# The softmax quotient of attention: from one long reciprocal in each block to twelve per partition by small transfers

## The chip, the core and the metric

The kernel runs on one core of a Trainium2 chip. The core's engines work side by side, each through its own instructions in order: TensorE (PE in the profile; its weight loads PEld), VectorE (DVE), ScalarE (ACT), GpSimd (POOL) and SyncE (SP), which here only issues transfers. The metric is the time of one execution in device microseconds; lower is better.

## What is computed

Attention with a hash mask over 2 batches x 8 heads, 768 positions, 64 columns a head; then two expert layers on its output, which the change doesn't touch.

```python
mask = q_bucket[:, :, :, None] == k_bucket[:, :, None, :]
scores = scale * np.matmul(q, k.transpose(0, 1, 3, 2))
scores = np.where(mask, scores, -1000000000.0)
scores = scores - np.max(scores, axis=-1, keepdims=True)
attn = np.exp(scores)
attn = attn / (np.sum(attn, axis=-1, keepdims=True) + 1e-09)
return np.matmul(attn, v).astype(np.float32)
```

The result, turned to x of 1536 x 512, goes through `h = x @ w_in`, a softmax-weighted h with a layer norm, `@ w_out`, and then a gate that sends each row to one of eight experts (two products each).

## The kernel before

Attention works on pairs of heads, j = 0 to 7, two heads side by side on the 128 partitions (64 each). A pair has two blocks, i = 0 and 1, of 384 queries each, and a block has six steps c, of 128 keys each. Scores are kept transposed: keys on partitions, queries along the row. In `run`, the order of the work is written out by hand:

- `score` (each c): TensorE makes scores of 128 keys x 384 queries of both heads into one of three score buffers in PSUM (`wide`), from high and low parts of Q and K and from F, rows that carry the hash mask and the negative row maximum (all L208); ScalarE takes the exponential (L246); on odd c GpSimd adds two of them (L250) and the sum so far (L252), the row sums in the making.
- `rowmax`: for a block to come, TensorE makes scores queries x keys in the same three buffers and VectorE reduces each to its maximum (L219). `submax` (at c = 1) joins the two halves of the keys (L224), clamps and negates (L226), and SP sends the result to one row of Fq by two transfers of 128 pieces (L231).
- at c = 1 of i = 0: `turn` (transposes of the next pair's Q and K, their high and low parts: L170 to L178), `av(j - 1, 1)` (P x V of the block before, L261), `hash` (L185, bits L190), `direct(j - 1, 1)`, `mask` (L197, L201), and SP's loads of V of pair j + 1 and Q and K of pair j + 2. At c = 1 of i = 1: `av(j, 0)`, `direct(j, 0)`, and one of seven clearings of the scratch tensor (SP).
- `direct` makes the quotient: TensorE sums the exponentials over partitions (L273); VectorE copies a column vb that lies beside the product (L280), adds EPS to the sums (L281), takes the reciprocal of all 128 x 384 (L282; within a head all 64 partitions hold the same row), and multiplies (L283, which reads the product in PSUM and adds vb).
- `extra`: the weights of the first expert layer come as float64 and are turned to float32 in 16 pieces, two instructions' turns at the end of every step c from the second block on: ScalarE scales (L392), VectorE shifts (L394), joins (L397) and sets the sign (L401), then ScalarE and GpSimd split into high and low parts (L411, L412; pieces 0 to 7) or ScalarE scales by g (L407; pieces 8 to 15). The transfer of the next piece (512 KB, ScalarE's queue, L376) is issued between two of them.

The three score buffers bind the engines together: TensorE can write the next scores only where VectorE (L219) or ScalarE (L246) has read a buffer.

Of the kernel before, what the change touches and what calls it, by code (L numbers as in the profile page):

```python
# [8 lines left out]
F32 = mybir.dt.float32  # L9
F32R = mybir.dt.float32r  # L10
BF16 = mybir.dt.bfloat16
AF = mybir.ActivationFunctionType
ALU = mybir.AluOpType
AX = mybir.AxisListType
PSUM = bass.MemoryType.PSUM

P = 128
S = 768
D = 64
NC = S // P  # L20
BIG = float(2 ** 40)
E = 8
EPS = 1e-9
NPT = 8
ROWM = 16
HW = S // 2
# [99 lines left out]
class Attention:  # L126
# [85 lines left out]
    def rowmax(self, j, i, c, kh):  # L212
        nc, st = self.nc, self.st[j]
        if (c, kh) == (0, 0):
            st["m", i] = self.sp.tile([P, 3, 2, 2], F32, tag="m", name="m")
        ps = self.wide()
        q, k = slice(i * HW + c, (i + 1) * HW, 3), slice(kh * HW, (kh + 1) * HW)
        self.both(ps, [(st[x + "q"][:, q], st[x + "k"][:, k]) for x in "HF"])
        nc.vector.tensor_reduce(out=st["m", i][:, c, :, kh], in_=ps, axis=AX.X, op=ALU.max)  # L219

    def submax(self, j, i):
        nc, st = self.nc, self.st[j]
        m = st["m", i]
        nc.vector.tensor_tensor(out=m[:, :, :, 0:1], in0=m[:, :, :, 0:1], in1=m[:, :, :, 1:2], op=ALU.max)  # L224
        mr = self.sp.tile([P, 2, 3, 1], F32R, tag="mr", name="mr")
        nc.vector.tensor_scalar(  # L226
            out=mr.rearrange("p h c o -> p c h o"), in0=m[:, :, :, 0:1], scalar1=-BIG / 2, scalar2=-1.0, op0=ALU.max, op1=ALU.mult
        )
        for h in range(2):
            r = D * h + ROWM  # L230
            nc.sync.dma_start(  # L231
                out=st["Fq"][r:r + 1, i * HW:(i + 1) * HW].bitcast(F32),
                in_=mr[:, h, :, 0].bitcast(F32),
            )
# [28 lines left out]
                    start=(c == 0), stop=(c == NC - 1), tile_position=(0, D * h),  # L263
                )

    def direct(self, j, i):
        nc, C, st = self.nc, self.C, self.st[j]
        b, hp = divmod(j, 4)
        ps = self.narrow()
        n = len(st["acc", i])  # L270
        for c in range(n):
            for h in range(2):
                nc.tensor.matmul(  # L273
                    ps[D * h:D * h + D, :], C["ones"], st["acc", i][c][:, h], start=(c == 0), stop=(c == n - 1),
                    tile_position=(0, D * h),
                )
        rb = self.ap.tile([P, HW], F32, tag="rb", name="rb", bufs=2)
        x = st["x", i]
        vb = self.sp.tile([P, 1], F32, tag="vb", name="vb")
        nc.vector.tensor_copy(vb, x[:, HW:HW + 1])  # L280
        nc.vector.tensor_scalar(out=rb, in0=ps, scalar1=EPS, scalar2=None, op0=ALU.add)  # L281
        nc.vector.reciprocal(out=rb, in_=rb)  # L282
        nc.vector.scalar_tensor_tensor(  # L283
            out=self.xT[:, b, hp, i * HW:(i + 1) * HW], in0=x[:, 0:HW], scalar=vb, in1=rb, op0=ALU.add, op1=ALU.mult
        )

    def run(self, n, extra, fills):
        self.last = (n - 1, 1)
        scan = [(j, i, c, kh) for j in range(n) for i in range(2) for c in range(3) for kh in range(2)]

        def scans(m):
            for x in scan[:m]:
                self.rowmax(*x)
            del scan[:m]

        self.turn(0)
        self.hash(0)
        self.mask(0)
        scans(NC)
        self.submax(0, 0)  # L300
        scans(3)
        half = [tuple(range(NC)), (0, 1, 2), (3, 4, 5)]
        for j in range(n):
            nx = j + 1 < n
            for i in range(2):
                more = nx or not i
                for c in range(NC):
                    self.score(j, i, c)
                    scans(((2, 1, 0, 1, 1, 1), (2, 1, 1, 1, 1, 0))[i][c])
                    if c == 1:  # L310
                        if nx or i == 0:
                            self.submax(*((j, 1) if i == 0 else (j + 1, 0)))
                        if i == 0:
                            if nx:
                                self.turn(j + 1)
                            if j:
                                self.av(j - 1, 1, half[0])
                            if nx:
                                self.hash(j + 1)
                            if j:  # L320
                                self.direct(j - 1, 1)
                                self.st.pop(j - 1)
                            if nx:
                                self.mask(j + 1)
                                if j:
                                    self.load(j + 1, "v")
                            if j + 2 < n:
                                self.load(j + 2, "qk")
                        else:
                            self.av(j, 0, half[0])  # L330
                            self.direct(j, 0)
                            if fills:
                                fills.pop(0)()
                    if c == 4 and (j, i) == self.last:
                        self.av(j, 1, half[1])
                    for _ in range(2):
                        if j or i:
                            next(extra, lambda: None)()
        for f in extra:
            f()  # L340
        self.av(n - 1, 1, half[2])
        self.direct(n - 1, 1)


class Weights:
# [10 lines left out]
    def steps(self, pool):  # L356
        nc = self.nc
        todo = [(0, k, h) for k in range(4) for h in range(2)] + [(1, f, 0) for f in range(8)]
        wide = self.src[0].dtype != F32
# [21 lines left out]
        def convert(n):  # L381
            m, k, h = todo[n]
            w = got[n]
            ops = []
            if wide:
                H, L = w[:, :, 1], w[:, :, 0]
                a = pool.tile([P, 512], F32, tag="w", name="w")
                w = self.wo[:, k, :] if m else a
                ai, wi = a.bitcast(I32), w.bitcast(I32)
                V = nc.vector  # L390
                ops = [
                    lambda: nc.scalar.activation(out=a, in_=H.bitcast(F32), func=AF.Copy, scale=2.0 ** -112),  # L392
                    lambda: None,
                    lambda: V.tensor_scalar(  # L394
                        out=ai, in0=ai, scalar1=4, scalar2=1, op0=ALU.logical_shift_left, op1=ALU.logical_shift_right
                    ),
                    lambda: V.scalar_tensor_tensor(  # L397
                        out=ai, in0=L, scalar=29, in1=ai, op0=ALU.logical_shift_right, op1=ALU.bitwise_or
                    ),
                    lambda: None,  # L400
                    lambda: V.scalar_tensor_tensor(  # L401
                        out=wi, in0=H, scalar=-(1 << 31), in1=ai, op0=ALU.bitwise_and, op1=ALU.bitwise_or
                    ),
                    lambda: None,
                ]
            if m:
                ops.append(lambda: nc.scalar.activation(out=w, in_=w, func=AF.Copy, scale=self.g[:, k:k + 1]))  # L407
            else:
                hi, lo = (x[:, k, h * 512:h * 512 + 512] for x in self.wi)
                ops += [  # L410
                    lambda: nc.scalar.copy(hi, w),  # L411
                    lambda: nc.gpsimd.tensor_tensor(out=lo, in0=w, in1=hi.bitcast(F32), op=ALU.subtract),  # L412
                ]
            return ops
# [1 line left out]
        load(0)  # L416
        yield
        for n in range(len(todo)):
            for t, f in enumerate(convert(n)):
                if t == 2:  # L420
                    load(n + 1)
                yield f
            if wide:
                yield from [lambda: None] * (2 if n < 8 else 3)
            if not wide:
                load(n + 1)


def apart(tc, group, ins, gap):
# [735 lines left out]
```

## Time and profile before

| | |
|---|---|
| median of 3 runs (lowest to highest) | 710.62 us (710.31 to 719.96) |
| the profiled execution | 709.09 us |
| its span, first to last instruction | 707.4 us |
| mean granted TensorE clock | 0.939 |
| busy share: TensorE, VectorE, ScalarE, GpSimd | 87%, 68%, 39%, 47% |
| attention stage, from the first row maximum to the first product of the expert layer | 16.4 to 327.0 us |

A line such as L282 is a line of the kernel's source. "Idle before" is time in which the engine did nothing just before the instruction, with what released it behind the arrow. The chain of waits is followed back from the last instruction: at each step to what released it. The granted clock of TensorE is a share of its full speed.

### The profile page before, as it was taken

To read this page: it belongs to the slowest core of one execution; us is meant where nothing else is said; L and a number is where in the kernel's file an instruction comes from. 1 tells how busy PE (TensorE), PEld (TensorE's weight loads), DVE (VectorE), ACT (ScalarE), POOL (GpSimd) and SP (SyncE) were. 2 spreads that over 40 slices of the span, in tenths; PEclk is the share of its full clock that TensorE was granted. 3 is DMA by queue.
4 is the path that set the end of the run, shared out by engine and by line. 5 is a ranking of instruction groups with operands and counts; after the bars stand their busy time and mean duration, and the time that the engine had idled before them with its cause. 6 is when DMAs were issued, how large, how long until landed. Compare 5 with 4: busy or idle time off the path is not lost.

```text
span 707.4 us, 10052 instructions
## 1 busy us (share of the span) xinstructions
PE 615.8 (87%) x3906; PEld 478.7 (68%) x3906; DVE 477.6 (68%) x825; ACT 272.5 (39%) x448; POOL 330.4 (47%) x267
## 2 busy tenths in 40 slices
PE   4788777987788796779699999998899999999995
PEld 2455554544455565556588888887699889988994
DVE  5877867886878877854876787775744664466540
ACT  2344335442525352333323232261343545454530
POOL 1164654865454535554610100333436966696651
PEclk9998989998979998899899999997999999999998
DMA  6141334343343421206000000200466458658400
GB/s 163 24 112 47 82 91 97 90 98 89 97 90 81 108 51 45 78 1 237 1 0 1 1 1 0 75 1 30 167 237 215 164 205 284 213 184 308 144 18 30
DMA packets 77367, 70.11 MB, mean 99 GB/s; under 512 B 46333, under 2 KB 55293, under 8 KB 77312
## 3 DMA queue, kind: packets, MB, share of 16 engines
q1 hardware_dynamic: 72608, 54.69, 26.4%
q10 hardware_dynamic: 2464, 8.39, 3.7%
q0 software_dynamic: 2240, 6.31, 2.5%
q8 instruction: 32, 0.52, 0.3%
q14 instruction: 23, 0.19, 0.1%
HBM read 55.64 MB, written 14.74 MB: 99 GB/s over the span
## 4 chain that ended last, share of the span: by engine, by line
PE 69%; DVE 20%; DMA 3%; POOL 2%; issue 2%; ACT 2%; SPq 1%; POOLq 0%; ACTq 0%; DVEq 0%
PE g L948 13%; PE o L970 13%; PE x L261 9%; PE ps L208 9%; PE y L497 8%; PE h L497 8%; DVE rb L282 4%; DVE m L219 4%; DVE w L397 3%; PE ps L170 2%; PE pm L273 2%; PE t L560 2%; DMA k<-in_k_dram 1%; DVE w L401 1%; DVE w L394 1%
## 5 line engine op out<-in xcount | busy, mean ns | idle before, releaser
L250 POOL TENSOR_TENSOR acc<-pt,pt 128x768 f32<-128x768 f32 x48 | 90.0, 1875 | 141.5 <-ACT pt L246 141.2
L888 POOL TENSOR_TENSOR wl<-ws,wh 128x512 fp32r<-128x512 f32 x80 | 113.5, 1454 | 71.0 <-ACT wh L886 70.5
L246 ACT ACTIVATE pt<-ps 128x768 f32<-128x768 f32 x96 | 76.4, 812 | 98.6 <-PE ps L208 98.6
L219 DVE TENSOR_REDUCE m<-ps 128x2 f32<-128x768 f32 x96 | 88.8, 950 | 25.0 <-PE ps L208 24.6
L886 ACT CAST wh<-ws 128x512 fp32r<-128x512 f32 x128 | 70.3, 618 | 6.0 <-POOL wl L888 4.4
L261 PE MATMUL x<-pt,v 128*64 128x385 f32 x384 | 68.6, 508 | 1.7 <-DVE xT L283 1.7
L208 PE MATMUL ps<-Hq,Hk 64*128 64x384 f32 x192 | 43.4, 447 | 30.5 <-DVE m L219 22.5
L208 PE MATMUL ps<-Hk,Hq 64*128 64x384 f32 x192 | 43.6, 448 | 24.7 <-DVE m L219 22.1
L888 DVE TENSOR_TENSOR wl<-ws,wh 128x512 fp32r<-128x512 f32 x48 | 57.0, 1214 | 11.3 <-ACT wh L886 11.0
L954 DVE SCALAR_TENSOR_TENSOR hl<-g,hh 128x512 fp32r<-128x512 f32 x32 | 22.1, 691 | 62.1 <-ACT hh L953 51.2
L252 POOL TENSOR_TENSOR acc<-acc 128x768 f32<-128x768 f32 x30 | 58.5, 1948 | 2.4
L208 PEld LDWEIGHTS ps<-Hq,Hk 64*128 64x128 f32 x192 | 20.5, 209 | 50.3 <-DVE m L219 27.3
L473 POOL TENSOR_TENSOR xl<-xT,xh 128x512 fp32r<-128x512 f32 x12 | 15.6, 1306 | 82.4 <-ACT xh L488 37.1
L953 ACT ACTIVATE hh<-g 128x512 fp32r<-128x512 f32 x32 | 19.2, 599 | 84.5 <-PE g L948 61.1
L261 PEld LDWEIGHTS x<-pt,v 128*64 128x64 f32 x384 | 27.0, 142 | 36.2 <-issue 35.7
L970 PE MATMUL o<-wh,hh 128*128 128x512 f32 x128 | 51.1, 399 | 0.0
L970 PE MATMUL o<-wl,hh 128*128 128x512 f32 x128 | 50.5, 394 | 0.0
L970 PE MATMUL o<-wh,hl 128*128 128x512 f32 x128 | 50.5, 394 | 0.0
L497 PE MATMUL h<-wi,xh 128*128 128x512 f32 x192 | 50.4, 405 | 0.0
L208 PEld LDWEIGHTS ps<-Hk,Hq 64*128 64x128 f32 x192 | 26.0, 265 | 34.8 <-DVE m L219 28.4
L497 PE MATMUL y<-wo,lh 128*128 128x512 f32 x192 | 47.2, 398 | 0.0
L948 PE MATMUL g<-xh,wh 128*128 128x256 f32 x256 | 41.2, 283 | 0.3 <-ACT xh L917 0.3
(214 smaller groups left out, 1332.5 us busy)
## 6 DMA issues: line engine op xcount, KB each, us to landing
ws<-in_moe_w_dram SPq DMA_DIRECT2D x32, 1024.0 KB
scratch<-zero SPq DMA_DIRECT2D x7, 1030.0 KB
r<-scratch SPq DMA_DIRECT2D x16, 257.5 KB
raw<-in_moe_w_in_dram ACTq DMA_DIRECT2D x8, 512.0 KB
raw<-in_moe_w_out_dram ACTq DMA_DIRECT2D x8, 512.0 KB
q<-in_q_dram SPq DMA_DIRECT2D x16, 192.0 KB
k<-in_k_dram SPq DMA_DIRECT2D x16, 192.0 KB
v<-in_v_dram SPq DMA_DIRECT2D x16, 192.0 KB
```

Of the source, the lines that this page charges most:

```text
L208: self.nc.tensor.matmul(ps[:, h], w[r], x[r], start=(n == 0), stop=(n == len(jobs) - 1), tile_position=(D * h, 0))
L219: nc.vector.tensor_reduce(out=st["m", i][:, c, :, kh], in_=ps, axis=AX.X, op=ALU.max)
L246: nc.scalar.activation(out=pt[:, :, 0:HW], in_=ps, func=AF.Exp, scale=0.125)
L250: nc.gpsimd.tensor_tensor(out=acc, in0=st["pt", i, c - 1][:, :, 0:HW], in1=pt[:, :, 0:HW], op=ALU.add)
L252: nc.gpsimd.tensor_tensor(out=acc, in0=parts.pop(), in1=acc, op=ALU.add)
L261: nc.tensor.matmul(st["x", i][D * h:D * h + D, 0:HW + 1], st["v"][:, c, h, :], st["pt", i, c][:, h, 0:HW + 1], start=(c == 0), stop=(c == ...
L282: nc.vector.reciprocal(out=rb, in_=rb)
L497: nc.tensor.matmul(ps, a[:, k, :], w[j](k), start=(n == 0), stop=(n == len(jobs) - 1))
L886: nc.scalar.copy(hi[:, k, :], t[:, k, :])
L888: eng.tensor_tensor(out=lo[:, k, :], in0=t[:, k, :], in1=hi[:, k, :].bitcast(F32), op=ALU.subtract)
L948: nc.tensor.matmul(ps[:, a, :], w[:, k, f * P:(f + 1) * P], x[:, k, :], start=(n == 0), stop=(n == 11))
L970: nc.tensor.matmul(st["o"][t], h[:, f, t * P:(t + 1) * P], w[:, f % 4, :], start=(f == 0 and n == 0), stop=(f == 7 and n == 2),)
```

## The change

Three parts, all in the attention stage.

The quotient. For pairs 0 to 6 `direct` is taken apart. `evac` copies vb and has ScalarE write the product plus vb from PSUM to SBUF (`xr`). `total` sums and adds EPS. `sums` does both halves of a pair one after the other, and after the second SP gathers the 2 x 768 sums, one partition of each head, to 128 partitions x 12 (`rc`). `recip`, at c = 4 of the next pair's i = 0, takes the reciprocal of these 12 columns; SP writes them to DRAM (`rd`) and reads them back by two broadcasts to 64 partitions each. `norm`, at c = 3 of the next pair's i = 1, multiplies 128 x 768 by 128 x 768. Pair 7 keeps a reciprocal of 128 x 384 in each block (`direct`).

The row maximum. L219 negates, and one scalar_tensor_tensor (two minima) stands for L224 and L226.

The conversions. A piece belongs to a block, from the first block on; the next piece's transfer is issued at the block's start. In i = 0 its instructions stand at the end of c = 0 (ScalarE), in c = 1 after `submax` (L394), and at the end of c = 2 (L397), 3 (L401), 4 and 5. In i = 1: c = 0 (ScalarE), then all three of VectorE in c = 1 between `av` and `evac`, then c = 2 and 3.

```diff
-        nc.vector.tensor_reduce(out=st["m", i][:, c, :, kh], in_=ps, axis=AX.X, op=ALU.max)
+        nc.vector.tensor_reduce(out=st["m", i][:, c, :, kh], in_=ps, axis=AX.X, op=ALU.max, negate=True)
...
-        nc.vector.tensor_tensor(out=m[:, :, :, 0:1], in0=m[:, :, :, 0:1], in1=m[:, :, :, 1:2], op=ALU.max)
         mr = self.sp.tile([P, 2, 3, 1], F32R, tag="mr", name="mr")
-        nc.vector.tensor_scalar(
-            out=mr.rearrange("p h c o -> p c h o"), in0=m[:, :, :, 0:1], scalar1=-BIG / 2, scalar2=-1.0, op0=ALU.max, op1=ALU.mult
+        nc.vector.scalar_tensor_tensor(
+            out=mr.rearrange("p h c o -> p c h o"), in0=m[:, :, :, 0:1], scalar=BIG / 2, in1=m[:, :, :, 1:2],
+            op0=ALU.min, op1=ALU.min,
         )
...
+    def evac(self, j, i):
+        nc, st = self.nc, self.st[j]
+        x = st["x", i]
+        vb = self.sp.tile([P, 1], F32, tag="vb", name="vb")
+        nc.vector.tensor_copy(vb, x[:, HW:HW + 1])
+        if i == 0:
+            st["xr"] = self.ap.tile([P, 2, HW], F32, tag="xr", name="xr", bufs=2)
+        nc.scalar.activation(out=st["xr"][:, i], in_=x[:, 0:HW], func=AF.Identity, bias=vb, scale=1.0)
+
+    def total(self, j, i):
...
+        if i == 0:
+            st["rb"] = self.ap.tile([P, 2, HW], F32, tag="rb", name="rb")
+        nc.vector.tensor_scalar(out=st["rb"][:, i], in0=ps, scalar1=EPS, scalar2=None, op0=ALU.add)
+
+    def sums(self, j, i):
+        nc, st = self.nc, self.st[j]
+        self.total(j, i)
+        if i:
+            st["rc"] = self.sp.tile([P, 12], F32, tag="rc", name="rc")
+            nc.sync.dma_start(out=st["rc"], in_=st["rb"][0:P:D].rearrange("p a n -> p (a n)"))
+
+    def recip(self, j):
+        nc, st = self.nc, self.st[j]
+        nc.vector.reciprocal(out=st["rc"], in_=st["rc"])
+        rd = self.tc.dram_tile([2, S], F32, name=f"rd{j}")
+        nc.sync.dma_start(out=rd.rearrange("h n -> (h n)").rearrange("(p t) -> p t", p=P), in_=st["rc"])
+        rb = st["rb"] = self.ap.tile([P, 2, HW], F32, tag="rd", name="rd")
+        for h in range(2):
+            nc.sync.dma_start(
+                out=rb[D * h:D * h + D].rearrange("p a n -> p (a n)"), in_=rd[h:h + 1].to_broadcast([D, S])
+            )
+
+    def norm(self, j):
+        b, hp = divmod(j, 4)
+        st = self.st.pop(j)
+        o = self.xT[:, b, hp, :].rearrange("p (a n) -> p a n", a=2)
+        self.nc.vector.tensor_tensor(out=o, in0=st["xr"], in1=st["rb"], op=ALU.mult)
+
+    def direct(self, j, i):
...
         nc.vector.reciprocal(out=rb, in_=rb)
-        nc.vector.scalar_tensor_tensor(
-            out=self.xT[:, b, hp, i * HW:(i + 1) * HW], in0=x[:, 0:HW], scalar=vb, in1=rb, op0=ALU.add, op1=ALU.mult
-        )
+        nc.vector.tensor_tensor(out=self.xT[:, b, hp, i * HW:(i + 1) * HW], in0=st["xr"][:, i], in1=rb, op=ALU.mult)
...
                         if i == 0:
+                            some(1)
                             if nx:
                                 self.turn(j + 1)
...
                             if j:
-                                self.direct(j - 1, 1)
-                                self.st.pop(j - 1)
+                                self.evac(j - 1, 1)
+                                self.sums(j - 1, 1)
...
                             self.av(j, 0, half[0])
-                            self.direct(j, 0)
+                            some(3)
+                            self.evac(j, 0)
+                            (self.sums if nx else self.direct)(j, 0)
                             if fills:
                                 fills.pop(0)()
+                    else:
+                        some(1)
+                    if j and (i, c) == (0, 4):
+                        self.recip(j - 1)
+                    if j and (i, c) == (1, 3):
+                        self.norm(j - 1)
                     if c == 4 and (j, i) == self.last:
                         self.av(j, 1, half[1])
-                    for _ in range(2):
-                        if j or i:
-                            next(extra, lambda: None)()
-        for f in extra:
-            f()
+                some(9)
```

`some(m)` issues the next m instructions of the block's piece.

## Rows read from the trace of the kernel before

**Rows 1.** Busy us by stretch: window, length, each engine, clock, DMA share, GB/s.

```profile
105.96:139.83 33.87, 28.81 (x226) 18.41 (x228) 27.40 (x34) 16.05 (x23) 20.52 (x12) 1.00 0.40 98
...
218.56:256.00 37.44, 31.36 (x226) 20.56 (x228) 31.26 (x34) 16.68 (x24) 17.69 (x10) 0.91 0.34 89
...
256.00:296.43 40.43, 30.86 (x215) 21.30 (x216) 30.14 (x33) 15.39 (x22) 18.61 (x11) 0.83 0.28 76
```

**Rows 2.** Chain of waits, attention stage: start us, length us, what.

```profile
47.68 2.56 DVE rb L282
...
63.72 4.03 PE x L261 x24
...
224.81 2.56 DVE rb L282
...
296.43 4.04 PE x L261 x24
...
316.57 2.56 DVE rb L282
```

**Rows 3.** Groups of instructions: total busy us, mean ns, idle before.

```profile
L219 DVE TENSOR_REDUCE m<-ps 128x2 f32<-128x768 f32 x96 | 88.8, 950 | 25.0 <-PE ps L208 24.6
...
L394 DVE TENSOR_SCALAR w<-w 128x512 int32<-128x512 int32 x16 | 15.6, 972 | 6.5 <-ACT w L392 6.5
...
L397 DVE SCALAR_TENSOR_TENSOR w<-raw,w 128x512 int32<-128x512 int32 x16 | 29.7, 1855 | 0.3
```

**Rows 4.** VectorE in order of time: start, length, instruction [idle before].

```profile
186.98 2.55 DVE L282 RECIPROCAL rb<-rb 128x384 f32<-128x384 f32 x1
...
218.12 1.53 DVE L224 TENSOR_TENSOR m<-m 128x6 f32<-128x6 f32 x1
...
223.44 0.62 DVE L190 TENSOR_SCALAR bits<-ps,thr 128x384 bf16<-128x384 f32 x1 [1.48 <-PE ps L185]
...
227.93 0.42 DVE L394 TENSOR_SCALAR w<-w 128x512 int32<-128x512 int32 x1
...
241.65 0.16 DVE L280 COPY vb<-x 128x1 f32<-128x1 f32 x1 [1.39 <-PE x L261]
...
242.30 0.56 DVE L281 TENSOR_SCALAR rb<-pm 128x384 f32<-128x384 f32 x1 [0.49 <-PE pm L273]
...
249.38 0.94 DVE L219 TENSOR_REDUCE m<-ps 128x2 f32<-128x768 f32 x1
...
262.25 2.55 DVE L282 RECIPROCAL rb<-rb 128x384 f32<-128x384 f32 x1
...
300.01 0.17 DVE L224 TENSOR_TENSOR m<-m 128x6 f32<-128x6 f32 x1
```

**Rows 5.** GpSimd in order of time, around 218.12.

```profile
217.81 1.82 POOL L250 TENSOR_TENSOR acc<-pt,pt 128x768 f32<-128x768 f32 x1
```

**Rows 6.** TensorE in order of time: after a gap, and undisturbed.

```profile
231.49 0.64 PE L208 MATMUL ps<-Hq,Hk 64*128 64x384 f32 x2 [2.64 <-DVE m L219]
...
242.63 0.35 PE L208 MATMUL ps<-Hq,Lk 64*128 64x384 f32 x2
```

**Rows 7.** SP's queue in order of time: issues of loads in one turn.

```profile
222.63 1.30 SPq L161 DMA_DIRECT2D v<-in_v_dram  x2
...
225.36 1.79 SPq L161 DMA_DIRECT2D k<-in_k_dram  x2
```

**Rows 8.** Chain of waits, the first row-maximum transfer.

```profile
22.89 0.54 SPq L231
...
23.54 2.02 DMA Fq<-mr
```

**Rows 9.** Groups of ScalarE, shapes apart.

```profile
L599 ACT COPY yT<-h 128x256 f32<-128x256 f32 x1 | 0.4, 372 | 0.2 <-PE h L598 0.2
...
L246 ACT ACTIVATE pt<-ps 128x768 f32<-128x768 f32 x96 | 76.4, 812 | 98.6 <-PE ps L208 98.6
```

**Rows 10.** Busy us in one microsecond, columns as in Rows 1.

```profile
231.00:232.00 1.00, 0.51 (x4) 0.51 (x6) 1.00 (x2) 0.00 (x0) 1.00 (x1) 0.79 0.21 46
```

More of the change, by code (lines that the diff above doesn't have):

```diff
@@ L264, in av @@
                 )
-    def direct(self, j, i):
+    def evac(self, j, i):
[7 more added lines that the diff above has]
+    def total(self, j, i):
         nc, C, st = self.nc, self.C, self.st[j]
-        b, hp = divmod(j, 4)
         ps = self.narrow()
@@ L276, in direct @@
                 )
[L277 to L281, printed above, removed]
+        if i == 0:
[23 more added lines that the diff above has]
+    def direct(self, j, i):
+        nc, st = self.nc, self.st[j]
+        b, hp = divmod(j, 4)
+        self.total(j, i)
+        rb = st["rb"][:, i]
         nc.vector.reciprocal(out=rb, in_=rb)
-        nc.vector.scalar_tensor_tensor(
-            out=self.xT[:, b, hp, i * HW:(i + 1) * HW], in0=x[:, 0:HW], scalar=vb, in1=rb, op0=ALU.add, op1=ALU.mult
-        )
+        nc.vector.tensor_tensor(out=self.xT[:, b, hp, i * HW:(i + 1) * HW], in0=st["xr"][:, i], in1=rb, op=ALU.mult)
     def run(self, n, extra, fills):
@@ L306, in run, with some @@
                 more = nx or not i
+                ops = next(extra, [])
+                def some(m):
+                    for f in ops[:m]:
+                        f()
+                    del ops[:m]
                 for c in range(NC):
@@ L330, in run @@
                             self.av(j, 0, half[0])
-                            self.direct(j, 0)
+                            some(3)
+                            self.evac(j, 0)
+                            (self.sums if nx else self.direct)(j, 0)
                             if fills:
                                 fills.pop(0)()
+                    else:
[4 more added lines that the diff above has]
+                        self.norm(j - 1)
                     if c == 4 and (j, i) == self.last:
                         self.av(j, 1, half[1])
-                    for _ in range(2):
-                        if j or i:
-                            next(extra, lambda: None)()
-        for f in extra:
-            f()
+                some(9)
         self.av(n - 1, 1, half[2])
+        self.evac(n - 1, 1)
         self.direct(n - 1, 1)
+        for ops in extra:
+            for f in ops:
+                f()
 class Weights:
@@ L392, in convert @@
                     lambda: nc.scalar.activation(out=a, in_=H.bitcast(F32), func=AF.Copy, scale=2.0 ** -112),
-                    lambda: None,
                     lambda: V.tensor_scalar(
@@ L399, in convert @@
                     ),
-                    lambda: None,
                     lambda: V.scalar_tensor_tensor(
@@ L403, in convert @@
                     ),
-                    lambda: None,
                 ]
@@ L418, in steps @@
         for n in range(len(todo)):
[L419 to L426, printed above, removed]
+            ops = convert(n)
+            load(n + 1)
+            yield ops
 def apart(tc, group, ins, gap):
```

## The prediction

> **What bounds the kernel now.** I first read the page's busy shares and its 40 slices, which say only that TensorE and VectorE are both busy most of the time in the first 327 us, the attention stage; nothing in the diff runs later. Then I read the chain of waits over that stage. From 47 to 317 us the same thing ends nearly every block: TensorE finishes P x V, then the row sums (L273), VectorE adds EPS (L281), takes the reciprocal of a 128x384 tile (L282, 2.56 us), and only then goes on to the weight conversions (L394, L397, L401) and the row maxima (L219) that TensorE's score buffers wait for; behind them the chain returns to TensorE. Twelve of the 16 reciprocals stand on that chain, the first at 47.68, the last at 316.57 [rows 2], so their length is paid, not hidden.
>
> One turn of the loop over head pairs j (two blocks, i = 0 and i = 1) goes from one P x V at the same place to the next. From j = 1's to j = 7's, 63.72 to 296.43, that is 232.7 us for six turns, 38.8 us each [rows 2]. In the turn 218.56 to 256.00 VectorE is busy 31.26 of 37.44 us, ScalarE 16.68 and GpSimd 17.69; TensorE shows 31.36, but at a mean granted clock of 0.91 [rows 1]. TensorE's clock has the levels 1.2 and 2.4 GHz, so 0.91 is about 18% of the turn, 6.7 us, at the lower one; at the upper all the time the same work would take some 3.4 us less, about 28 us. VectorE is the nearest bound, and TensorE waits for it: 2.64 us idle before 231.49, behind L219, and the matmuls right after the gap take 0.64 us where undisturbed ones take 0.35 [rows 6]. The turn 105.96 to 139.83 kept the clock at 1.00 and took 33.87 us, the one at 0.83 took 40.43 [rows 1].
>
> **The change, part by part.** I sum over the stage; a half is one block's quotient of 384 columns.
>
> *Reciprocal and product leave the blocks.* Fourteen halves (all but those of j = 7) no longer run L282 and L283 there. From the start of a reciprocal to the next VectorE instruction it is 3.12 us (224.81 to 227.93) [rows 2, 4]. Eleven of the 14 are on the chain. Two more, such as the one at 262.25, stand in a run of VectorE without a gap [rows 4], and I count them. The one at 186.98 [rows 4] lies beside TensorE's work, and I don't. 13 x 3.12 = 40.6 us off.
>
> *Conversions move.* In i = 1 blocks all three VectorE conversions now stand between the row maximum and the quotient, while TensorE does P x V. Before, VectorE idled there 1.39 us before vb and 0.49 before L281 [rows 4]: 1.88 us of conversion is hidden in seven blocks (j = 0 to 6), 13.2 us off. The rest of the three (L394 and L397 alone have means of 0.97 and 1.86 [rows 3]) delays vb as much as it delayed the next row maximum before, so it counts nothing. In i = 0 blocks L394 moves ahead of the split of Q and K, where VectorE has an idle 1.48 us before the hash bits [rows 4]; its mean 0.97 fits: 7 x 0.97 = 6.8 off. The weight DMAs on ScalarE's queue come a few instructions earlier; the buffer they wait for was read a block before, so nothing. ScalarE's and GpSimd's shares of a conversion keep their length; those engines are half idle [rows 1], nothing.
>
> *The one long product (norm).* Seven 128x768 products of two SBUF tensors. No row shows one. The nearest of that size is L219, 0.95 us [rows 3]. But a VectorE instruction with two SBUF inputs waits while GpSimd's sum runs: the six-element L224 took 0.17 us with GpSimd idle and 1.53 at 218.12, when it ended with GpSimd's sum that ran 217.81 to 219.63 [rows 4, 5]. So norm costs 0.95 to 0.95 + 1.82 = 2.8. GpSimd is busy about half the time, and its sums of c = 3 start beside norm: I take the middle, 1.9, so 13.3 us on.
>
> [...]
>
> *Reciprocal of 12 per partition.* About the shortest VectorE instruction, 0.17 us [rows 4]: 7 x 0.17 = 1.2 on. It waits for a small transfer that SP issues right after L281. The small row-maximum transfer took 2.02 us to land after its issue (0.54) [rows 8]; between L281 and the reciprocal VectorE has L397, L401 and two L219 (1.9 us the two, 1.86 the mean of L397 [rows 3]), over 3 us. I take no wait; up to 1 us x 7 if it is late.
>
> *Evacuation on ScalarE.* A new 128x384 Identity. Between 0.37 us for 256 columns and 0.81 for 768 [rows 9]: an estimate of 0.48. It comes behind vb and ahead of the next exponentials. I put half on the chain: 14 x 0.25 = 3.5 on; ends 0 and 6.7. The trace has a single table load and I expect none added.
>
> *Row maximum.* L226 goes, L224 becomes a scalar_tensor_tensor of the same size and inputs, so with the same wait; both lie in stretches where VectorE then idles [rows 4]. Nothing. Negating in L219 costs nothing: the same reduction.
>
> *SP's queue.* Per turn it gains four transfers, in order: gather (behind L281), after the q, k and v loads the write of the 768 x 2 quotients, then two broadcasts that must wait until the write has landed. Queued behind: the next row maxima (L231) and the clearing of scratch. The time from L281 to norm's slot is 26.1 us now (from just before the reciprocal at 224.81 to the end of the row maximum of c = 3, 249.38 + 0.94 [rows 2, 4]) and some 18.5 when a turn is nearly 8 us shorter. The chain of transfers, an estimate from rows: gather issue 0.5, six load issues 4.5 (222.63 to 227.15 [rows 7]), 4.1 until the loads have drained (the DMA share falls to 0.21 by 231.2 to 232 [rows 10]), 2.0 to land the write; then two issues 1.1, landing 2.0, and 393 KB at the loads' pace (1.18 MB from 222.63 to about 231.2) 2.9: 17.1 us. It fits by 1.4 us, and the row maxima that follow are wanted a block later. Nothing.
>
> *Clock.* The lower level comes after gaps like that before 231.49, and those gaps are VectorE's lateness. If the clock came back whole it would give 7 x 3.4 = 24 us. The turn at clock 1.00 speaks for its being on the path; TensorE's 28 us are still below the turn's new length, and new gaps can open. I count half, 12 us off, and keep 0 and 24 for the range.
>
> **Sum:** 40.6 + 13.2 + 6.8 - 13.3 - 1.2 - 3.5 + 12 = 54.6 us off the profiled execution's 709.1 (span 707.4): 654.5. The median of the runs shown is 710.6, 1.5 above it: 656 as a median. A turn becomes 38.8 - 54.6/7 = 31 us, above TensorE's 28 and above VectorE's new work (31.3 - 2 x 3.1 + 2.1 = 27.2), so neither is passed.
>
> **The rivals.**
>
> *The small transfers come late (B).* SP's queue is in order and the loads' 256-byte pieces are ahead. If the broadcasts land 3 us after norm's turn, VectorE stands still and TensorE behind it: 7 x 3 = 21, so 677. For it: the margin is only 1.4 us; against: nothing on the queue waits for VectorE in between except the 12 reciprocals.
>
> *GpSimd becomes the bound (C).* Its 17.7 us then fill 31 instead of 37.4, and norm holds it up. L394's mean exceeds its undisturbed length by 0.55 (0.97 against 0.42), L224's worst by 1.36 [rows 3, 4]; with GpSimd busy a fifth more of the time, such waits grow by about 0.1 us on each of eight instructions, 0.8 us a turn, and norm at its full 2.8: 5.6 + 6.3 = 12 on; with the gaps that this leaves, the clock's 12 don't come either: 680.
>
> *More than the sum (D).* The clock comes back whole and norm is met at 0.95: 12 + 6.7 more, 637; a turn is then 28.4 us, where TensorE binds.
>
> *It moves to another wait (F).* The row maxima come earlier, but the three score buffers wait for ScalarE's exponentials instead, whose queue now holds vb's follower. If two thirds of the gain go back: 692. Against it, ScalarE is under half busy.
>
> *Slower (E).* The same chain of transfers, far longer: if from L281 to norm it takes 30 us, norm is 11.5 us late in each of seven turns: 80.5 - 54.6 = 26 on, 737. It decides from 18.5 + 54.6/7 = about 26 us. That needs the transfers to take 26 us where I estimate 17; the clearing of scratch, the only large transfer that could do it, is issued behind them.
>
> By the Trainium skill's page "DMA: Bandwidth & Descriptors", section "Two DMAs through the same engine are not ordered", the broadcasts can't rely on the queue's order and must wait for the write's semaphore. No row of before has such a pair to show it.
>
> **How the numbers follow.** The forecast 0.53 (own range 642 to 670); B 0.17; C 0.13; D 0.05; F 0.07; E 0.05. A difference under 2%, 14 us, is about what a measurement of this kernel can't tell from none: faster is the first four, 0.88; F mostly within, 0.07; E slower, 0.05. The range 636 to 688 takes in B, C and D and leaves out F and E, with a little of the tails. The ends of the costs give it too: the 11 reciprocals on the chain alone, norm at 2.8, the Identity whole, no conversion hidden and no clock leave 34.3 - 19.6 - 1.2 - 6.7 = 7; all at its best gives 43.7 + 13.2 + 6.8 - 6.7 - 1.2 + 24 = 80; I cut both.
>
> **What would show it.** Right: no 128x384 reciprocal before j = 7; a turn near 31 us and its clock above 0.95; L397 in i = 1 beside P x V; norm with 1 to 3 us; idle of VectorE before the 12 reciprocals and norm near nothing. Wrong: VectorE idle before norm or the small reciprocal with a DMA as releaser (B, E); POOL ending the wait of L273 (C); the wait of TensorE for exponentials grown where that for L219 shrank (F).

## The result and the profile after

The changed kernel takes 661.4 us (median of 4 runs, 658.3 to 662.9), 0.931 of the kernel before's 710.5; over all four of its runs beside it the ratio is 0.924 (95% interval 0.915 to 0.934). The profiled execution took 662.0 with a span of 660.2, against 709.1 and 707.4: 47.2 us less. The attention stage ends at 278.6 instead of 327.0 us, 48.4 us earlier; what comes after it takes as long as before, to about 1 us. On every chip used here some runs of the kernel before are disturbed (719 to 721 us at a lower granted clock, against 706 to 713), so it is the others that times here and below are compared with.

Busy us by stretch in the changed kernel, from one P x V to the next as in [rows 1], with the same columns:

```profile
16.37:62.24 45.87, 38.08 (x272) 27.82 (x274) 33.81 (x40) 19.48 (x27) 19.94 (x12) 0.93 0.34 76
...
95.08:127.95 32.87, 28.13 (x227) 18.25 (x228) 23.69 (x29) 16.95 (x24) 22.01 (x13) 1.00 0.47 114
...
192.12:223.49 31.37, 27.94 (x227) 18.28 (x228) 24.64 (x30) 17.15 (x25) 19.31 (x11) 1.00 0.50 119
223.49:253.13 29.64, 26.39 (x214) 16.98 (x216) 22.97 (x28) 16.33 (x24) 17.67 (x10) 1.00 0.38 99
```

Beside [rows 1]: a full turn is 29.6 to 32.9 us where the three of [rows 1] are 33.9 to 40.4, and the clock column, third from the end, reads 1.00 in every full turn. VectorE is busy 23 to 25 us of a turn instead of 27 to 31, GpSimd 18 to 22. The six turns together take 190.9 us, 31.8 each, against 232.7 and 38.8. The first line is the exception: the stretch before the first full turn became only 1.5 us shorter, at a clock of 0.93.

The chain of waits over one of the later turns, those of pieces 8 to 15 (start us, length us, what):

```profile
198.49 2.03 PE ps L208 x20
...
200.54 0.96 DVE m L219
201.50 2.17 DVE wo L449
203.66 0.88 DVE m L219
...
212.56 2.58 PE ps L208 x23
...
216.04 2.39 DVE xT L311
218.43 0.88 DVE m L219
...
221.96 1.53 PE ps L170 x12
```

Where [rows 2] have a reciprocal of 2.56 us in each block, this has one conversion (L449) in the i = 0 block and, in the i = 1 block, the long product L311, which is norm. Between them the chain is mostly TensorE's; in the turns of pieces 0 to 7 GpSimd's sums stand on it as well (e6). The groups of VectorE that are new or that changed (total busy us, mean ns, idle before):

```profile
L449 DVE SCALAR_TENSOR_TENSOR w<-raw,w 128x512 int32<-128x512 int32 x8 | 17.3, 2168 | 0.1
...
L311 DVE TENSOR_TENSOR xT<-xr,rd 128x768 f32<-128x768 f32 x7 | 15.0, 2143 | 0.0
...
L443 DVE TENSOR_SCALAR w<-w 128x512 int32<-128x512 int32 x16 | 12.1, 753 | 10.6 <-ACT w L442 10.6
...
L446 DVE SCALAR_TENSOR_TENSOR w<-raw,w 128x512 int32<-128x512 int32 x16 | 12.5, 780 | 0.3
...
L298 DVE RECIPROCAL rc<-rc 128x12 f32<-128x12 f32 x7 | 1.5, 214 | 0.7 <-DMA rc<-rb 0.7
```

L298, the reciprocal of 12 per partition, is 0.21 us, and VectorE waited for its transfer once, 0.7 us, in all seven. L311 has a mean of 2.14 us and no idle before it. L446, the join, has a mean of 0.78 us where L397 had 1.86 [rows 3].

### The profile page after: what moved, and what is told of

Same layout as the page of the kernel before. It is cut to its first block, busy times and chain, and to the rows that moved or that the text cites. A ratio compares the mean times of both kernels' runs of the same rounds, so it can differ in the third digit from the quotient of the medians.

```text
span 660.2 us, 10112 instructions
## 1 busy us (share of the span) xinstructions
PE 596.9 (90%) x3906; PEld 464.9 (70%) x3906; DVE 434.4 (66%) x795; ACT 280.0 (42%) x464; POOL 333.1 (50%) x267
## 3 DMA queue, kind: packets, MB, share of 16 engines
q1 hardware_dynamic: 75646, 57.53, 30.5%
## 4 chain that ended last, share of the span: by engine, by line
PE 67%; DVE 14%; POOL 8%; ACT 5%; issue 3%; DMA 2%; SPq 0%; POOLq 0%; ACTq 0%; DVEq 0%
PE g L990 14%; PE o L1012 14%; PE h L539 9%; PE y L539 9%; PE x L261 7%; PE ps L208 6%; DVE m L219 4%; POOL acc L252 3%; POOL acc L250 3%; DVE xT L311 2%; ACT pt L246 2%; PE t L602 2%; PE ps L170 2%; PE pm L281 2%; DVE w L449 1%
## 5 line engine op out<-in xcount | busy, mean ns | idle before, releaser
L219 DVE TENSOR_REDUCE m<-ps 128x2 f32<-128x768 f32 x96 | 88.8, 948 | 34.6 <-PE ps L208 34.4
L261 PE MATMUL x<-pt,v 128*64 128x385 f32 x384 | 65.8, 491 | 0.0
L252 POOL TENSOR_TENSOR acc<-acc 128x768 f32<-128x768 f32 x30 | 61.2, 2042 | 2.4
L208 PE MATMUL ps<-Hq,Hk 64*128 64x384 f32 x192 | 38.0, 391 | 12.6 <-DVE m L219 10.5
L261 PEld LDWEIGHTS x<-pt,v 128*64 128x64 f32 x384 | 26.1, 137 | 31.7 <-issue 30.5
L539 PEld LDWEIGHTS h<-wi,xh 128*128 128x128 f32 x192 | 35.9, 194 | 8.0 <-ACT xh L530 0.6
```

Source lines behind the costliest of these rows:

```text
L208: self.nc.tensor.matmul(ps[:, h], w[r], x[r], start=(n == 0), stop=(n == len(jobs) - 1), tile_position=(D * h, 0))
L252: nc.gpsimd.tensor_tensor(out=acc, in0=parts.pop(), in1=acc, op=ALU.add)
L261: nc.tensor.matmul(st["x", i][D * h:D * h + D, 0:HW + 1], st["v"][:, c, h, :], st["pt", i, c][:, h, 0:HW + 1], start=(c == 0), stop=(c == ...
L539: nc.tensor.matmul(ps, a[:, k, :], w[j](k), start=(n == 0), stop=(n == len(jobs) - 1))
```

## The experiments

The kernel before is called B, the changed one C. Differences are between medians in us, B's median being that on the same chip (707.4 for e1 to e4, 709.5 for e5 to e8, 708.8 for e9 to e11, 710.5 for e12); a ratio to B stands with its 95% interval where that was computed against the same runs of B.

**e1, the quotient alone.** B with the diff's quotient; conversions and row maximum as in B (the diff is against C).

```diff
-                ops = next(extra, [])
+                    for _ in range(2):
+                        if j or i:
+                            next(extra, lambda: None)()
```

> The quotient part alone on the kernel before (conversions spread over the steps as before, row maximum as before). Theory 1, the parts add up as in the forecast's sum: 40.6 - 13.3 - 1.2 - 3.5 = 22.6 us off, and up to half of the clock's 24: 676 to 688 us. Rival, the parts overlap (the conversions, still spread between the row maxima, take the reciprocal's place as what VectorE is late with, and the clock stays low): 695 us or more, clock in the turns still near 0.9.

687.6, 19.8 below B (ratio 0.971, 0.967 to 0.975). The prediction's terms for this part, without any clock, are 40.6 - 13.3 - 1.2 - 3.5 = 22.6; the run comes out 2.8 short of them. The time is theory 1's, the clock the rival's. Two of its turns:

```profile
99.05:137.85 38.80, 31.34 (x226) 19.94 (x225) 29.44 (x32) 17.23 (x25) 23.97 (x13) 0.92 0.39 97
...
252.31:280.09 27.78, 26.54 (x214) 17.05 (x213) 21.61 (x30) 16.31 (x24) 15.89 (x9) 1.00 0.49 125
```

Most turns are like the first line, 35 to 41 us at a clock of 0.90 to 0.95; only the last full one comes out at 27.8 with the clock at 1.00.

**e2, the conversions alone.** B with the conversions placed as in C; `direct` and row maximum as in B (the diff is against C).

```diff
-                                self.evac(j - 1, 1)
-                                self.sums(j - 1, 1)
+                                self.direct(j - 1, 1)
+                                self.st.pop(j - 1)
```

> The placing of the conversions alone on the kernel before (reciprocal of 128x384 in each block, row maximum as before). Theory 1: 13.2 + 6.8 = 20 us off and up to half of the clock's 24: 678 to 691 us. Rival, the gain hangs on the reciprocal being gone: in i = 1 the conversions now stand ahead of the reciprocal, the product with V is over before VectorE is through, and the gain is under 10 us: 700 or more.

690.4, 17.0 below B (0.974, 0.968 to 0.980): theory 1, and near the sum's 13.2 + 6.8 = 20.0. The reciprocal need not be gone for the conversions to be hidden. VectorE's idle time in front of vb and L281, while TensorE makes P x V and the row sums, is 25.4 us over B's stage, 8.5 in e2 and 3.6 in C: that is the room the conversions went into. The clock stayed low; a late turn:

```profile
209.68:246.68 37.00, 31.91 (x225) 21.52 (x224) 29.34 (x34) 16.17 (x23) 18.54 (x11) 0.86 0.36 90
```

**e3, the row maximum alone.** B with L219 negated and the one scalar_tensor_tensor.

```diff
-        nc.vector.tensor_reduce(out=st["m", i][:, c, :, kh], in_=ps, axis=AX.X, op=ALU.max)
+        nc.vector.tensor_reduce(out=st["m", i][:, c, :, kh], in_=ps, axis=AX.X, op=ALU.max, negate=True)
...
-        nc.vector.tensor_tensor(out=m[:, :, :, 0:1], in0=m[:, :, :, 0:1], in1=m[:, :, :, 1:2], op=ALU.max)
...
+        nc.vector.scalar_tensor_tensor(
```

> The row maximum's change alone on the kernel before. Theory 1, it lies in VectorE's idle: 710 us, no change that can be measured. Rival, it is on the path: 16 x 0.16 us of L226 and some of its fixed gaps, 3 to 4 us off, 707.

One of its four runs can be compared: 707.8, within B's 705.9 to 710.3 on that chip. No difference shows, but a single run can't rule out 2 or 3 us.

**e4, norm under P x V.** C with the long product a block later, ahead of P x V and the row sums.

```diff
                             some(1)
                             if nx:
                                 self.turn(j + 1)
+                            if j > 1:
+                                self.norm(j - 2)
...
-                    if j and (i, c) == (1, 3):
+                    if not nx and (i, c) == (1, 3):
                         self.norm(j - 1)
```

> The changed kernel with the long product norm of pair j - 2 moved to i = 0 of turn j, right behind the split of Q and K, where TensorE makes P x V, VectorE idles 1.44 us before the hash bits and GpSimd is between its sums; only the last pair's stays. Theory 1, norm's 2.3 to 2.4 us with its wait for GpSimd are on the path in each of six turns: 11 to 15 us off 661, 646 to 650, and norm itself takes about 0.95 us there. Rival, another wait (GpSimd's sums, the exponentials) stands right behind it: under 5 us off, 656 or more.

653.4, 54.0 below B (0.923, 0.919 to 0.927), where C is 49.0 below its B (e5). Five us, at the edge of the rival's number, in spite of norm being what theory 1 said it would be there. VectorE in order of time:

```profile
190.55 0.95 DVE L178 TENSOR_TENSOR Lk<-ps,Hk 128x768 fp32r<-128x768 f32 x1
191.41 1.01 DVE L311 TENSOR_TENSOR xT<-xr,rd 128x768 f32<-128x768 f32 x1
192.94 0.62 DVE L190 TENSOR_SCALAR bits<-ps,thr 128x384 bf16<-128x384 f32 x1 [0.51 <-PE ps L185]
```

In five of its six new places norm takes 0.95 to 1.0 us (in the last, 2.56) and eats an idle that the bits had before them (0.51 left of 1.44). The turns of the later pieces went from 31.4 to 29.5, those of pieces 0 to 7 only from 32.85 to 32.25: there another wait stood right behind, which e6 names.

**e5, C again**, unchanged, for the chip of e6 to e8.

> The changed kernel itself once more, on the chip and beside the runs that e6 and e7 are compared with: 658 to 663 us as on record, all whole turns at a granted clock of 1.00.

660.5, 49.0 below B (0.931), with the turns of the trace on record to 0.06 us.

**e6, norm under P x V and a second buffer for the conversions.** e4 with:

```diff
-                a = pool.tile([P, 512], F32, tag="w", name="w")
+                a = pool.tile([P, 512], F32, tag="w", name="w", bufs=2)
```

> e4 (norm under P x V) and a second buffer for the conversions' tile w. In pieces 0 to 7 ScalarE's first step (L442) waits until GpSimd has made the low part (L459) out of the one w buffer, and VectorE's three conversions, vb and the exponentials come behind it. Theory 1, that buffer makes the turns of pieces 0 to 7 longer than the later ones (32.25 against 29.5 us in e4): with two buffers they come near 30, 5 to 8 us off e4, 645 to 648. Rival, GpSimd's own load is the bound there (its extra 1.28 us each block): the turns stay at 31.5 to 32.3 and the time within 2 us of e4's 653.

644.0, 65.5 below B (0.908), the lowest median of all. In C the chain of waits reads, over a turn of pieces 0 to 7:

```profile
110.16 1.81 POOL acc L252
111.97 1.24 POOL wi L459
...
113.23 0.69 ACT w L442
...
113.95 0.44 DVE w L443
...
114.42 0.70 DVE w L446
...
115.14 2.23 DVE w L449
...
117.48 0.58 ACT xr L273
```

GpSimd's row sums, then its low part of the weights (L459); ScalarE's next conversion (L442) starts 0.02 us after that ends, because there is one w; behind it stand VectorE's three conversions, vb (L270) and the Identity (L273). With two buffers, a turn of pieces 0 to 7 and one after them:

```profile
89.63:120.11 30.48, 27.88 (x226) 18.40 (x225) 25.32 (x30) 16.84 (x25) 21.24 (x13) 1.00 0.48 123
...
180.52:210.03 29.51, 27.75 (x225) 18.33 (x225) 22.54 (x30) 17.14 (x25) 18.64 (x11) 1.00 0.49 126
```

30.5 against 32.25 in e4, GpSimd's busy time in the turn as before (21.2 us): theory 1. GpSimd's part of the chain of waits over two such turns fell from 27.6 us in e4 to 7.7. It was the buffer that made GpSimd's queue a bound, not its load.

**e7, norm earlier.** C with norm in i = 1 at c = 1, behind `sums`; one run.

```diff
                             (self.sums if nx else self.direct)(j, 0)
+                            if j:
+                                self.norm(j - 1)
...
-                    if j and (i, c) == (1, 3):
-                        self.norm(j - 1)
```

> The changed kernel with norm moved ahead, to c = 1 of i = 1 right behind the sums, about 3 us before its place, to see when the broadcasts land. The forecast's 17.1 us from the end of L287 to their landing would make it wait 1 to 2 us (there are about 15 us). Theory 1, the margin is real but small: VectorE idles there with the broadcast as releaser, and the kernel is 0 to 10 us slower than the changed one. Rival, the transfers are much quicker than estimated: no idle before norm, and the time within 3 us of 661.

651.8, 8.7 below C's median on the same chip (e5): the rival, and more than it said. VectorE in order of time, then GpSimd, then SP's queue:

```profile
200.90 0.21 DVE L298 RECIPROCAL rc<-rc 128x12 f32<-128x12 f32 x1
...
209.04 0.56 DVE L287 TENSOR_SCALAR rb<-pm 128x384 f32<-128x384 f32 x1
209.52 0.95 DVE L311 TENSOR_TENSOR xT<-xr,rd 128x768 f32<-128x768 f32 x1
```

```profile
212.21 1.84 POOL L250 TENSOR_TENSOR acc<-pt,pt 128x768 f32<-128x768 f32 x1 [4.96 <-ACT pt L246]
```

```profile
201.14 0.33 SPq L300 DMA_DIRECT2D rd<-rc  x1
205.15 1.13 SPq L303 DMA_DIRECT2D rd<-rd  x2
```

Norm starts with no idle before it at 209.52, so the broadcasts, issued from 205.15 on, had landed 14.7 us at most after the end of L287 (194.80); I had estimated 17.1. And it takes 0.95 us in six of the seven, where GpSimd is between two sums (idle for 4.96 us before 212.21); the last takes 2.58.

**e8, B with its gaps filled** (in front of the waits, at the end of c = 3 and 4):

```diff
+    def keep(self, n):
+        ps = self.narrow()
+        for _ in range(n):
+            self.nc.tensor.matmul(ps, self.C["onesb"], self.C["tab"].rearrange("p g c -> p (g c)")[:, 0:HW], start=True, stop=True)
...
+                    if c in (3, 4):
+                        self.keep(6)
```

> The kernel before with six more 128x384 matmuls at the end of steps c = 3 and c = 4 of every block, into a PSUM tile that nobody reads, on constants: they run where TensorE would stand idle for VectorE (about 1 us each time at full clock). Nothing else is changed. Theory 1, the lower clock after such gaps is on the path and is a part of its own of the change's gain: the turns' clock goes up to 0.97 or more and the kernel is 5 to 20 us faster, 688 to 703. Rival, the path is VectorE's whatever the clock: 706 to 712, or slower by the added matmuls, up to 16 x 2 us.

714.8, 5.3 above B (1.009, 1.004 to 1.013), with the clock up (mean 0.958 against 0.939):

```profile
108.77:145.34 36.57, 32.87 (x250) 20.47 (x249) 30.76 (x36) 16.20 (x23) 21.64 (x13) 1.00 0.39 91
...
261.90:301.47 39.57, 33.71 (x238) 21.17 (x237) 30.23 (x34) 15.04 (x22) 17.75 (x11) 0.91 0.28 77
```

The same two turns of B took 33.87 us at 1.00 and 40.43 at 0.83 [rows 1]; here they take 36.57 at 1.00 and 39.57 at 0.91. Over the six turns it is 232.4 us against 232.7. Summed over the chain of waits of these turns, TensorE's share fell from 121.9 to 105.8 us and VectorE's rose from 84.4 to 97.0. A higher clock gave TensorE back 16 us, and it spent 13 of them waiting for VectorE: the rival. The added matmuls themselves stand on that chain for 4.2 us, so at most about 4 us of a gain are covered up by them. The filling gave back about half of the clock that was missing: over the six turns it is 0.95 on average, in B 0.90.

**e9, norm at e7's place and two w buffers.** C with the edit of e7 and the one line of e6.

```diff
+                            if j:
+                                self.norm(j - 1)
...
-                a = pool.tile([P, 512], F32, tag="w", name="w")
+                a = pool.tile([P, 512], F32, tag="w", name="w", bufs=2)
```

> e7 (norm right behind the sums of c = 1, i = 1) and two buffers for the conversions' tile w. Theory 1, e6's norm often met GpSimd's sum (median 2.07 us), while at e7's place GpSimd is between sums: norm at 0.95 us, 2 to 6 us off e6's 644, 638 to 642. Rival, TensorE is the bound by now (28 us a turn at full clock): within 2 us of e6.

645.4, 63.4 below B (0.911, 0.908 to 0.914). All seven norms take 0.946 to 0.957 us, but it is no better than e6: turns of 30.4 and 29.5 us, TensorE busy 27.8 of them. By its number the rival, though most of the chain is TensorE's only in the later turns (24 of 29.5 us there, 14 of 30.4 in those of pieces 0 to 7).

**e10, e1 with its gaps filled as in e8.**

```diff
+                    if c in (3, 4):
+                        self.keep(6)
```

> e1 (the quotient alone, turns at a clock of 0.90 to 0.95 but for the last) with six idle-time matmuls at the end of c = 3 and c = 4 as in e8. e1 and e2 took off 20 and 18.5 us, together 38.5, the whole change about 48. Theory 1, the missing 10 us are the clock, which comes back only when VectorE no longer sets the pace: with the gaps filled the turns' clock reaches 0.98 or more and the kernel is 5 to 12 us faster than e1's 687.6, in spite of the added matmuls. Rival, the missing part is waits (conversions between row maxima, GpSimd's sums): 686 or more, up to 700.

692.2, 16.6 below B (0.976, 0.972 to 0.980) where e1 is 19.8 below (and e2 17.0, not 18.5): by its number the rival. But the added matmuls themselves stand on the chain of waits for 14.1 us of the stage, so what the higher clock (0.968 against 0.954) gave back may be as large as 11 us. It doesn't settle it.

**e11, the evacuation on VectorE.** C with L273 as a VectorE instruction:

```diff
-        nc.scalar.activation(out=st["xr"][:, i], in_=x[:, 0:HW], func=AF.Identity, bias=vb, scale=1.0)
+        nc.vector.tensor_scalar(out=st["xr"][:, i], in0=x[:, 0:HW], scalar1=vb, scalar2=None, op0=ALU.add)
```

> The changed kernel with the product's evacuation (plus vb) on VectorE instead of ScalarE's Identity. Theory 1, VectorE is still on the path in half of the steps and ScalarE's Identity costs less there: 14 x 0.56 (L287's length, same size) less the 3.5 us that the forecast gave the Identity, 2 to 8 us slower than 661. Rival, the exponentials that stand behind the Identity, which waits for vb, are the path: up to 4 us faster.

654.9, 53.9 below B (0.923, 0.919 to 0.927): about 5 us better than C, a little more than the rival said. But its turns after piece 7 are those of C (31.3), and the gain lies in the turns of pieces 0 to 7 (31.6 against 32.85), where norm had dropped to 1.25 to 1.32 us, and in the first stretch (44.2 against 45.9), where there is no norm.

**e12, e9 with the evacuation on VectorE**, to part the two.

```diff
-        nc.scalar.activation(out=st["xr"][:, i], in_=x[:, 0:HW], func=AF.Identity, bias=vb, scale=1.0)
+        nc.vector.tensor_scalar(out=st["xr"][:, i], in0=x[:, 0:HW], scalar1=vb, scalar2=None, op0=ALU.add)
```

> e9 with the evacuation on VectorE as in e11. e11 took 5 to 6 us off the changed kernel. Theory 1, that was the Identity itself (the exponentials stand behind it on ScalarE): then it comes off here as well, 638 to 641. Rival, e11's gain is norm's: its later start let norm miss GpSimd's sums in the turns of pieces 0 to 7 (L311's median 1.32 us there against 2.3); in e9 norm never meets them, so nothing is left to gain: 643 to 648.

649.7, 60.8 below B (0.914): 2.6 us less of a gain than e9's 63.4, turns of 31.0 and 30.0 against 30.4 and 29.5. With norm out of GpSimd's way, VectorE's version (0.62 us) is the dearer one. So most of e11's gain was norm's (what the first stretch gained is not explained), and with norm and the buffer put right ScalarE is the better engine by 2.6 us.

## Why the prediction came out as it did

The forecast was 656 us, the time is 661.4; in the spans the sum said 54.6 off and 47.2 came. The path was the one that was named, and the likeliest case held. By its steps:

- *Reciprocal and product leave the blocks, with norm, the small reciprocal and the Identity.* Together 22.6 in the sum, 19.8 alone in e1. Right, with two terms off: norm was put at 1.9 and has a mean of 2.14; the Identity was put at 0.48 and takes 0.58 us, though on the chain it is 3.6 us in all where the sum had 3.5.
- *Conversions move.* 20.0 in the sum, 17.0 alone in e2, and VectorE's idle under P x V filled as said.
- *Row maximum.* Nothing, and e3 shows nothing, to 2 or 3 us.
- *Norm waits for GpSimd.* Right in kind, but the middle was too low: six of the seven met a sum and took 2.29 to 2.40 us. In the turn shown it started at 216.04 beside GpSimd's sum:

```profile
216.04 2.39 DVE L311 TENSOR_TENSOR xT<-xr,rd 128x768 f32<-128x768 f32 x1
```

```profile
215.77 1.85 POOL L250 TENSOR_TENSOR acc<-pt,pt 128x768 f32<-128x768 f32 x1 [4.96 <-ACT pt L246]
```

  It ended 0.81 us after that sum's end (217.62), and where GpSimd was idle it took 0.95 (e4, e7, e9). The Trainium skill's page "SBUF — State Buffer", section "Who interferes with whom", is borne out by both: two SBUF inputs against a GpSimd instruction that reads SBUF, and the later one waits to the other's end. The place at c = 3, just where ScalarE's second exponential lets GpSimd start, was the worst of the three tried; e7's is 8.7 us better (one run).
- *SP's queue.* Right that VectorE doesn't wait there. The broadcasts do wait on the queue for the write: in the lines of e7 they are issued 4.0 us after it (205.15 against 201.14). The margin was larger than said (at most 14.7 us in e7, of 17.7 from L287 to norm in C), so rivals B and E had less behind them than I gave them.
- *Clock.* This step failed in its reasoning. I read the turn at clock 1.00 (33.9 us) against the one at 0.83 (40.4) as the clock's doing, and counted half of 24 us. e8 gave B back half of its missing clock and gained nothing, or some 4 us at most behind its added matmuls: as far as e8 goes, a low clock was there the mark of waiting for VectorE and cost little of its own. In C the clock did come back whole in all six full turns, as the result of the other steps. e1 and e2 leave 49.0 - 19.8 - 17.0 = 12 us that only both parts together bring, and the sum's 12 for the clock is that size; but whether these 12 us are the clock's or those of waits that one part alone leaves standing, e10 doesn't decide. That stays open, and the agreement in size confirms nothing.
- *What the sum lacked.* GpSimd and the single w. "ScalarE's and GpSimd's shares of a conversion keep their length; those engines are half idle, nothing" is the sentence that was wrong. In a shorter block the end of GpSimd's low part met the start of the next piece: 1.5 us in each of the three turns of pieces 0 to 7 beside the later ones, and most of the gain that the first stretch didn't have (43.2 us in e6 against 45.9). GpSimd's share of the chain of waits over the stage grew from 12.7 to 48.2 us. Rival C named the engine, but for norm's sake and not for the buffer's. Three turns at 1.5, norm's 0.24 more in each of seven and the first stretch's 2.7 make 8.9 us, about the 7.4 by which the sum was too large.

The chain of waits over the whole attention stage, summed by engine (us; the rest is transfers and issuing), shows the exchange:

| | stage | TensorE | VectorE | GpSimd | ScalarE | rest |
|---|---|---|---|---|---|---|
| B | 310.5 | 155.2 | 110.6 | 12.7 | 9.6 | 22.4 |
| e1, quotient alone | 290.9 | 157.1 | 64.9 | 26.4 | 25.4 | 17.1 |
| e2, conversions alone | 294.3 | 131.6 | 125.4 | 18.7 | 10.7 | 7.9 |
| C | 262.1 | 111.8 | 62.1 | 48.2 | 26.8 | 13.2 |

The quotient takes 46 us from VectorE's share, while GpSimd's and ScalarE's rise by 30; the conversions take 24 from TensorE's, since VectorE stands idle for 8.5 us instead of 25.4 while TensorE makes P x V and the row sums, and VectorE's rises by 15; only with both does TensorE's share fall by 43.

Part of what only both bring shows in the length of the conversions, a change that the sum put at nothing. The join took up to 2.3 us where it met GpSimd's sums and 0.68 to 0.69 where it met none: over 1.2 us in 14 of the 16 pieces in B, in nine in e1, eight in e2 and one in C. All conversions of VectorE together stand on the chain with 37.5 us in B, 29.1 in e1, 37.4 in e2 and 19.9 in C, so 9 us of the drop come only with both. No run tests by itself whether these are 9 of the open 12 us.

## What to carry to other kernels

A long instruction that ends nearly every block on the chain was worth about its full length here, less what the next queue in line took (19.8 us in e1 where the sum had 22.6): price that queue too, and above all its single buffers, for the time that the blocks will have afterwards. Of two stretches that differ in time and in TensorE's clock, the clock may be only the mark of the wait; fill the gaps with idle matmuls before a gain is counted for it. An elementwise product of two SBUF tensors on VectorE belongs where GpSimd is between instructions: the same product took 0.95 or 2.4 us by its place alone, and with norm moved and a second w buffer this kernel runs in 644 to 645 us (e6, e9) instead of 661.

## What had not been expected of the hardware

The small transfers were quicker than the sum of the rows read beforehand: gather, reciprocal, write to DRAM and broadcast back, with 1.2 MB of loads issued between, took at most 14.7 us (e7), and VectorE waited for the gather 0.7 us in seven turns. And a raised clock can leave the time of a kernel where it was: in e8 TensorE's 16 us on the chain came back as 13 of VectorE's. A single input in SBUF did not keep a VectorE instruction clear of GpSimd either: in B the shift (L394), w from w, took 0.42 us ahead of a sum (227.93 [rows 4]) and 1.82 beside one that ran from 265.08 to 266.92, ending 0.27 after it:

```profile
265.37 1.82 DVE L394 TENSOR_SCALAR w<-w 128x512 int32<-128x512 int32 x1
```
